# Attention and feed-forward on one core: the first batch's q and k loaded with four tokens in a partition and turned by their place in the group; SP's times in the planner's list as traced

## The chip, the core and the metric

The kernel runs on one core of one Trainium2 chip. The metric is the device time of one execution in microseconds, the median of several. A core has a matrix engine (TensorE, here PE, with its weight loads as PEld), VectorE (DVE), ScalarE (ACT), GpSimd (POOL), and SyncE (SP), which issues every DMA of this kernel. Each takes its instructions in the order of its own list. 16 DMA engines move the bytes. All operands are float32.

## The reference: what is computed

For each of 8 batches and 8 heads (576 tokens, head size 64), two attentions are added: one over q, k and v averaged over groups of four tokens (144 groups), whose result is repeated for the four tokens, and a local one in which a token sees the tokens at a distance below four. The sum, as rows of 512, goes through a layer norm and a feed-forward of 512 to 2048 to 512, and is added to the result.

```
q_d = q.reshape(B, H, Sd, 4, D).mean(axis=3)          # k_d, v_d likewise, Sd = 144
out_up = np.repeat(sm_attn(q_d, k_d, v_d), 4, axis=2)
mask = np.abs(pos[:, None] - pos[None, :]) < 4
out_local = softmax(where(mask, q @ k.T / sqrt(D), -1e9)) @ v
x = (out_up + out_local) as [B, S, H * D]
return x + relu(layernorm(x) * g_ln @ w_ch1) @ w_ch2
```

The two weight matrices arrive as 64-bit numbers and are turned into pairs of float32r tiles (hi and lo) on the chip.

## The kernel before, in words

**Stages.** The 4608 rows of x are cut into 18 chunks of 256 rows. A chunk is normed (`norm`), turned (px), split into xh and xlo, and then goes through 8 pairs of weight blocks (`ffn`): matmuls into h (L996), relu and split into hh and hl, matmuls into acc (L1019). The weights, 16 blocks of w1 and of w2, are loaded (L347, L352) and converted (cva, hi, lo) once, beside the first two chunks. Ahead of a chunk stands the attention of its batch: five windows of local attention (`local`, two strips of 58 tokens each, with overlap 64 rows), and four pairs of heads of pooled attention (`pooled_pair`).

**The first batch** (`own`, b = 0). Each of its five windows loads q and k as rows of tokens: for each, two DMAs of 64 rows with 8 runs of 256 bytes a row (`load_rows`, L428). PE turns a window with four transposes of 128x128 each (L458) into a PSUM tile, DVE adds groups of four columns there (`sums`, L480) into gsq and gsk, which are q and k of the pooled attention, and ACT copies the tile to SBUF (L465). Then come scores (ls), the softmax (lmx, la), its transpose (lt, at), the product with v (lv) and the division (xl). Pooled attention goes over qbdg, gs, gmx, ag, gt, agt and gv to od. Four tiles of x are made from xl and od by matmuls with 0/1 matrices (ex), and then normed. v of the pooled attention comes by its own loads (raw0v, raw1v: 72 rows, four heads with 1 KiB runs) and two additions on POOL; v of the windows goes into four tiles vwin. Windows 5 and 6 (of batch 1) use `load_rows` too; later ones use loads of blocks, DVE transposes, and moves of xl into x in pieces of up to 58 rows (L662).

**What sets the order.** `Plan` is given every step with an engine, a duration, what it depends on, a due time, and what it takes and gives of three kinds of rooms: SBUF tiles of 2 KiB a partition ("u", 88 of them), staging tiles and 8 PSUM banks ("a"). `order()` lists the steps as engines and rooms come free on its own clock, and the program is written out in that order, one list per engine; the durations in it order the work and do nothing else. T0, C1 and CHUNK set the due times of the feed-forward's pairs, W0 and W_GAP those of the weights, `rate` and `kb` the pace at which it believes bytes to land. Where the list leaves PE idle in its first 150 us, dummy transposes of the identity (L197) are put in.

Of the kernel before, what the change touches and what calls it, by code (L numbers as in the profile page):

```python
# [22 lines left out]
class Plan:  # L23
# [116 lines left out]
def attention_then_ffn(  # L140
# [129 lines left out]

    T0 = 35
    C1 = 5
    CHUNK = 55
    PACE = CHUNK / NPR

# [43 lines left out]
    U, A, STG = (("u", 1),), (("a", 1),), (("stg", 1),)  # L319
    DMA, LAT, W_AHEAD = 0.5, 2.9, 40  # L320

# [15 lines left out]
    def weights(which, f):  # L337
# [64 lines left out]
    chosen, own_moves = {}, []  # L402
    last_local = SimpleNamespace(v=[None] * NVW)

    def local(i):
# [44 lines left out]
        own = b < NPB  # L450
        for src, nm in ((q, "q"), (k, "k")):
            if by_pe:

                def turn(nm=nm):
                    p = psa(f"l{nm}{i}")
                    x.p[nm] = p
                    for pr in range(NPAIR):
                        nc.tensor.transpose(  # L458
                            p[:, pr * P : (pr + 1) * P],
                            x.raw[nm][:, 2 * pr : 2 * pr + 2].rearrange("p h d -> p (h d)"), ident,  # L460
                        )
# [6 lines left out]
                def sums(nm=nm):  # L468

                    for par in range(2):  # L470
                        t0 = window_start(w, par)
                        g0, g1 = (-(-(NQ * (2 * w + p)) // FACTOR) for p in (par, par + 1))
                        g1 = min(g1, SD)
                        c0 = 64 * par + FACTOR * g0 - t0
                        p = x.p[nm].rearrange("p (c t) -> p c t", c=NPAIR)
                        for hg in range(2):
                            key = (b, hg, nm)
                            if key not in gsum:
                                gsum[key] = unit([P, 2, SD], f"gs{nm}{b}_{hg}")
                            nc.vector.tensor_reduce(  # L480
                                out=gsum[key][:, :, g0:g1],
                                in_=p[:, 2 * hg : 2 * hg + 2, c0 : c0 + FACTOR * (g1 - g0)]
                                .rearrange("p c (g r) -> p c g r", r=FACTOR),
                                axis=AX.X, op=ALU.add,
                            )

                t = add("SP", 1.46, lambda src=src, nm=nm: load_rows(src, nm), (), due - 12.0, take=U,
                        lag=LAT, kb=256, ahead=AHEAD)
                t = add("PE", 0.43, turn, (t,), due - 8.0, take=A, give=U)
                if own:  # L490
                    t = add("DVE", 4 * dve(120), sums, [t] + gsum_done.get((b, nm), []), due - 8.0,
                            take=() if w else (("u", 2),))
                    gsum_done.setdefault((b, nm), []).append(t)
                turned.append(add("ACT", act(512), turn_out, (t,), due - 8.0, take=U, give=A))
            else:

                def turn(nm=nm):
                    t = unit([P, H, 64], f"l{nm}t{i}")
                    nc.vector.transpose(
                        t.rearrange("p h j -> p (h j)"), x.raw[nm].rearrange("p h j d -> p (h j d)")  # L500
                    )
                    setattr(x, nm + "t", t)

                ts = []
                for jb in range(2):
                    ts.append(add("SP", 4 * DMA, lambda src=src, nm=nm, jb=jb: load_blocks(src, nm, jb), ts,
                                  due - 14.0, take=() if jb else U, lag=LAT, kb=128, ahead=AHEAD))
                turned.append(add("DVE", dve(512), turn, ts, due - 8.0, take=U, give=U))
        vt = add("SP", 4 * DMA, load_v, (last_local.v[i % NVW],), due - 8.0, lag=LAT, kb=256, ahead=AHEAD)

        def scores_by_pair():
# [4 lines left out]
            for h2 in range(2):  # L516
                nc.tensor.matmul(
                    x.ps[h2], lhsT=ident_b, rhs=mask_b.unsqueeze(1).broadcast_to([P, NPAIR, 64]),
                    start=True, stop=False,
                )  # L520
            for pr in range(NPAIR):
                for h2 in range(2):
                    ds = slice(64 * h2, 64 * h2 + 64)
                    for par in range(2):
                        hs = slice(64 * par, 64 * par + 64)
                        nc.tensor.matmul(
                            x.ps[h2][hs, pr], lhsT=x.qt[ds, pr, hs], rhs=x.kt[ds, pr, hs],
                            start=False, stop=pr == NPAIR - 1,
# [77 lines left out]
        def divided(h2, eng):  # L606
# [7 lines left out]
            for pr in range(NPAIR):  # L614
# [3 lines left out]
        t = add("PE", 0.75, scores_by_pair if by_pe else scores_by_block, turned, due - 6.0,  # L618
                take=(("a", 2),), give=(("u", 2),))
        if not by_pe:  # L620
# [30 lines left out]
        for e, (n, p0, r0, m, par) in enumerate(moves):  # L651

            def move(n=n, p0=p0, r0=r0, m=m, par=par):
# [7 lines left out]
                for h2 in range(2):  # L661
# [4 lines left out]

            t = add("SP", DMA if by_pe else 2 * DMA, move, outs, due + 1.0, take=() if n in piece else U,
                    give=U if e == len(moves) - 1 else (), lag=LAT, kb=116)
# [13 lines left out]
    def pooled_half(b, hg):  # L682
# [6 lines left out]
        if own:  # L689
            ready["q"], ready["k"] = gsum_done[b, "q"], gsum_done[b, "k"]  # L690
        for nm, src in (("v", v),) if own else (("q", q), ("k", k), ("v", v)):
            for half in range(2):
# [23 lines left out]
                by_dve = b == 0 and nm == "k"  # L716
                t = add("SP", 0.82, load, (), due - 4.0, take=STG, lag=LAT, kb=288, ahead=AHEAD)
                t = add(
# [8 lines left out]
    def pooled_pair(b, hg, pr, x, ready):  # L727
# [121 lines left out]
        od_done.append(t)  # L849
        t = add("SP", DMA, keep, (t,), due, lag=LAT)  # L850
        ud_done.setdefault(b, []).append(t)
# [4 lines left out]
    def norm(n):  # L856
# [105 lines left out]
        else:  # L962
            t = add("SP", DMA * len(rows), load_up, [d for _, _, b, _ in rows for d in ud_done[b]], due - 4.0,
                    take=U, lag=LAT, kb=256, ahead=12.0)
# [95 lines left out]
    choice_done = plan.add("POOL", 4.0, make_choice, (), 10.0, take=U)  # L1060
    spread_done = plan.add("POOL", 2.5, make_spread, (choice_done,), 20.0, take=U)
    for i in range(NPB * NWIN):
        local(i)
# [52 lines left out]
```

## Time and profile before

| what | us |
|---|---|
| three runs: median, lowest, highest | 1064.73, 1063.45, 1066.62 |
| profiled execution, its own time | 1069.35 |
| span of its profile | 1067.0 |
| mean granted clock | 0.990 |

All views quoted below are of that one execution, in microseconds from the start of its span. Its own time is 2.35 us longer than the span and 4.62 longer than the median of the runs. The page cuts the span into 40 slices of 26.7 us; the digits are the busy share in tenths, PEclk the granted clock of TensorE:

```profile
PE   8897899989999999999999999999989999999998
DVE  7589954634353534444444443545434454534211
ACT  5575632413332222132222221223222222222110
PEclk9898999999999999999999999999999999999999
DMA  7788445535433533344354434243442443201000
GB/s 156 214 230 287 129 106 123 146 80 114 88 86 82 119 82 92 69 94 97 77 118 95 106 78 114 42 130 74 109 90 66 87 87 76 62 27 32 9 20 20
```

In a row of the groups, "out<-in" are the tiles written and read, behind the bar stand the busy time, the mean time of one in ns, and how long the engine had been idle just before, with what ended that. In the chain and the timeline a row gives start, length, engine, line, and how many instructions are merged.

### The profile page before, as it was taken

To read this page: it belongs to the slowest core of one execution; us is meant where nothing else is said; L and a number is where in the kernel's file an instruction comes from. 1 tells how busy PE (TensorE), PEld (TensorE's weight loads), DVE (VectorE), ACT (ScalarE), POOL (GpSimd) and SP (SyncE) were. 2 spreads that over 40 slices of the span, in tenths; PEclk is the share of its full clock that TensorE was granted. 3 is DMA by queue.
4 is the path that set the end of the run, shared out by engine and by line. 5 is a ranking of instruction groups with operands and counts; after the bars stand their busy time and mean duration, and the time that the engine had idled before them with its cause. 6 is when DMAs were issued, how large, how long until landed. Compare 5 with 4: busy or idle time off the path is not lost.

```text
span 1067.0 us, 23720 instructions
## 1 busy us (share of the span) xinstructions
PE 1039.3 (97%) x9280; PEld 932.2 (87%) x9280; DVE 509.5 (48%) x1307; ACT 313.2 (29%) x856; POOL 268.7 (25%) x286
## 2 busy tenths in 40 slices
PE   8897899989999999999999999999989999999998
PEld 8786789979999888889898989898989989888997
DVE  7589954634353534444444443545434454534211
ACT  5575632413332222132222221223222222222110
POOL 4233546323105221231224150142301400000000
PEclk9898999999999999999999999999999999999999
DMA  7788445535433533344354434243442443201000
GB/s 156 214 230 287 129 106 123 146 80 114 88 86 82 119 82 92 69 94 97 77 118 95 106 78 114 42 130 74 109 90 66 87 87 76 62 27 32 9 20 20
DMA packets 289295, 104.33 MB, mean 98 GB/s; under 512 B 237945, under 2 KB 276089, under 8 KB 289185
## 3 DMA queue, kind: packets, MB, share of 16 engines
q1 hardware_dynamic: 289185, 102.83, 40.7%
q8 instruction: 73, 1.20, 0.5%
q14 instruction: 37, 0.30, 0.1%
HBM read 82.58 MB, written 11.80 MB: 88 GB/s over the span
## 4 chain that ended last, share of the span: by engine, by line
PE 87%; DMA 4%; DVE 4%; SPq 2%; ACT 1%; issue 1%; POOL 0%; DVEq 0%; ACTq 0%; POOLq 0%
PE h L996 36%; PE acc L1019 35%; PE gv L802 3%; DMA s<-in_moe_w_ch_dram 3%; PE lv L596 2%; PE gs L766 2%; PE ls L540 2%; PE lt L575 1%; PE px L923 1%; PE gt L785 1%; SPq L428 1%; DVE cva L370 1%; DMA x<-xl 1%; PE gq L739 1%; DVE lo L383 1%
## 5 line engine op out<-in xcount | busy, mean ns | idle before, releaser
L1019 PE MATMUL acc<-hi,hl 128*128 128x512 f32 x576 | 238.2, 413 | 5.3 <-DVE hl L1007 5.3
L1019 PE MATMUL acc<-lo,hh 128*128 128x512 f32 x576 | 228.2, 396 | 0.0
L1019 PE MATMUL acc<-hi,hh 128*128 128x512 f32 x576 | 226.2, 393 | 0.0
L1003 ACT ACTIVATE hh<-h 128x512 fp32r<-128x512 f32 x144 | 86.2, 599 | 437.8 <-PE h L996 393.6
L1007 DVE SCALAR_TENSOR_TENSOR hl<-h,hh 128x512 fp32r<-128x512 f32 x144 | 98.9, 687 | 222.3 <-ACT hh L1003 214.7
L996 PE MATMUL h<-xh,lo 128*128 128x256 f32 x1152 | 193.2, 290 | 0.0
L996 PE MATMUL h<-xlo,hi 128*128 128x256 f32 x1152 | 185.3, 283 | 0.0
L996 PE MATMUL h<-xh,hi 128*128 128x256 f32 x1152 | 185.1, 283 | 0.0
L996 PEld LDWEIGHTS h<-xh,lo 128*128 128x128 f32 x1152 | 168.4, 190 | 16.9 <-POOL lo L383 0.2
L996 PEld LDWEIGHTS h<-xlo,hi 128*128 128x128 f32 x1152 | 159.1, 192 | 0.0
L996 PEld LDWEIGHTS h<-xh,hi 128*128 128x128 f32 x1152 | 158.6, 191 | 0.0
L896 POOL TENSOR_TENSOR x<-x,up 128x512 f32<-128x512 f32 x32 | 41.2, 1289 | 416.6 <-DMA x<-xl 310.9
L1019 PEld LDWEIGHTS acc<-hi,hh 128*128 128x128 f32 x576 | 109.0, 189 | 25.3
L1019 PEld LDWEIGHTS acc<-hi,hl 128*128 128x128 f32 x576 | 109.8, 191 | 22.0 <-DVE hl L1007 6.4
L1019 PEld LDWEIGHTS acc<-lo,hh 128*128 128x128 f32 x576 | 109.9, 191 | 12.5
L930 ACT ACTIVATE xh<-px,gain 128x128 fp32r<-128x128 f32 x144 | 43.6, 372 | 77.1 <-PE px L923 47.7
L940 DVE SCALAR_TENSOR_TENSOR xlo<-px,gain,xh 128x128 fp32r<-128x128 f32 x144 | 42.7, 344 | 34.7 <-ACT xh L930 34.5
L904 DVE BATCH_NORM_STATS2 st<-x 128x6 f32<-128x512 f32 x32 | 21.9, 686 | 47.1 <-POOL x L896 46.0
L779 ACT ACTIVATE ag<-gs,gmx 96x144 f32<-96x144 f32 x96 | 28.9, 373 | 42.9 <-DVE gmx L771 42.7
L1027 DVE SCALAR_TENSOR_TENSOR x<-acc,x 128x512 f32<-128x512 f32 x36 | 24.4, 688 | 35.3 <-PE acc L1019 35.3
L546 DVE TENSOR_TENSOR ls<-ls,mask 128x256 f32<-128x256 f32 x66 | 26.6, 424 | 27.2 <-PE ls L540 27.2
L802 PEld LDWEIGHTS gv<-vd,agt 72*72 72x72 f32 x512 | 37.2, 145 | 1.4
(191 smaller groups left out, 1156.8 us busy)
## 6 DMA issues: line engine op xcount, KB each, us to landing
s<-in_moe_w_ch_dram SPq DMA_DIRECT2D x64, 256.0 KB
vwin<-in_v_dram SPq DMA_DIRECT2D x160, 64.0 KB
out_dram<-x SPq DMA_DIRECT2D x36, 256.0 KB
qr<-in_q_dram SPq DMA_DIRECT2D x264, 32.0 KB
kr<-in_k_dram SPq DMA_DIRECT2D x264, 32.0 KB
up<-ud SPq DMA_DIRECT2D x28, 256.0 KB
x<-xl SPq DMA_DIRECT2D x66, 58.0 KB
ud<-od SPq DMA_DIRECT2D x32, 72.0 KB
```

The lines of the kernel that those rows point to most:

```text
L546: nc.vector.tensor_add(x.ps[n], x.ps[n], mask.unsqueeze(1).broadcast_to([P, NPAIR, 64]))
L779: nc.scalar.activation(y.a[:, c], y.ps[:, c], AF.Exp, scale=POOLED_SCALE, bias=y.mx[:, c : c + 1])
L802: nc.tensor.matmul(y.pv[:, qh, h2], lhsT=y.at[kh][:, h2, qh * GH : (qh + 1) * GH], rhs=vd[:, kh, 2 * pr + h2], start=kh == 0, stop=kh == 1,)
L896: nc.gpsimd.tensor_add(xt[n], xt[n], x.up)
L904: nc.vector.bn_stats(st, x.up if by_pe else xt[n])
L930: nc.scalar.activation(xh[c][i][:, k, j * P : (j + 1) * P], pxt[n][:, kc], AF.Copy, scale=gain[:, kc : kc + 1])
L940: nc.vector.scalar_tensor_tensor(out=xlo[c][i][:, k, ts], in0=pxt[n][:, kc], scalar=gain[:, kc : kc + 1], in1=xh[c][i][:, k, ts].bitcast(F ...
L996: nc.tensor.matmul(ph[c, p][:, fi], lhsT=wt[:, kc], rhs=xx[kc // 2][:, kc % 2], start=n == 0, stop=n == 3 * KC - 1)
L1003: nc.scalar.activation(hh[c, p], ph[c, p], AF.Relu)
L1007: nc.vector.scalar_tensor_tensor(out=hl[c, p].rearrange("p c t -> p (c t)"), in0=ph[c, p].rearrange("p c t -> p (c t)"), scalar=0.0, in1=h ...
L1019: nc.tensor.matmul(acc[c][j], lhsT=lt[:, fi, ts], rhs=rt, start=p == 0 and fi == 0 and n == 0, stop=p == NPR - 1 and fi == 1 and n == 2,)
L1027: nc.vector.scalar_tensor_tensor(out=x, in0=acc[c][j], scalar=1.0 + 2.0**-23, in1=x, op0=ALU.mult, op1=ALU.add)
```

## The change

**q and k of the first batch.** They are no longer loaded by window. `own_half` cuts the 144 groups of four tokens into two halves that overlap by three groups: groups 0 to 73 (74 of them) and 71 to 143 (73). For each pair of heads, each half, and each of q and k one DMA brings a group into a partition: 74 or 73 partitions, for each of two heads one run of 1 KiB (four tokens of 64). That makes 16 DMAs of 148 or 146 KiB where there were 20 of 128 KiB. PE turns the tile with eight matmuls against the identity, one for each place in the group and each head, written to PSUM at every fourth column, so that the tokens stand in order; DVE adds groups of four columns (288 at a time, to 72 sums), ACT copies 296 or 292 columns into an SBUF tile that stays until the last window that needs it. A window's scores then read 64 columns out of these tiles (`own_piece`). Each pooled half waits for the sums of its own four heads.

**The planner's numbers.** T0, CHUNK, W0, rate, LAT and the SP durations and sizes (kb) of all loads are set anew.

```
-        self.rate, self.moved = 245.0, 0.0
+        self.rate, self.moved = 260.0, 0.0
...
-    T0 = 35
+    T0 = 30
-    CHUNK = 55
+    CHUNK = 54
-    W0, W_GAP = 40, 13
+    W0, W_GAP = 30, 13
-    DMA, LAT, W_AHEAD = 0.5, 2.9, 40
+    DMA, LAT, W_AHEAD, W_LAG = 0.5, 2.5, 40, 1.5
...
-        t = add("SP", 2 * DMA, load, (), due, take=(("u", 3),), lag=LAT, kb=512, ahead=W_AHEAD)
+        t = add("SP", 1.3, load, (), due, take=(("u", 3),), lag=LAT + W_LAG, kb=512, ahead=W_AHEAD)
...
+    OWN_G = ((0, GH + 2), (GH - 1, SD))
+    def own_half(b, half):
+        g0, g1 = OWN_G[half]
+        ng = g1 - g0
+        for e, (nm, src, pr) in enumerate((nm, src, pr) for pr in range(NPAIR) for nm, src in (("q", q), ("k", k))):
...
+                x.raw = unit([P, 2, FACTOR, D], f"{nm}o{b}_{pr}_{half}")[:ng]
+                nc.sync.dma_start(
+                    x.raw.rearrange("p h r d -> p h (r d)"),
+                    src[b, 2 * pr : 2 * pr + 2, FACTOR * g0 : FACTOR * g1].rearrange("h (g r) d -> g h (r d)", r=FACTOR),
+                )
...
+                for r in range(FACTOR):
+                    for h2 in range(2):
+                        nc.tensor.matmul(
+                            x.p[64 * h2 : 64 * h2 + 64, :, r], lhsT=x.raw[:, h2, r], rhs=ident[:ng, :ng],
+                            start=True, stop=True,
+                        )
...
+            t = add("SP", 0.5, load, (), due - 4.0, take=U, lag=LAT, kb=147, ahead=AHEAD)
+            t = add("PE", 0.45, turn, (t,), due, take=A, give=U)
...
-        for src, nm in ((q, "q"), (k, "k")):
+        for src, nm in () if own else ((q, "q"), (k, "k")):
...
-            ready["q"], ready["k"] = gsum_done[b, "q"], gsum_done[b, "k"]
+            ready["q"], ready["k"] = list(gsum_done[b, hg, "q"]), list(gsum_done[b, hg, "k"])
```

**What moves in the lists.** First SP, from its first loads on; qn and kn are a window's q and k, qo and ko those of a pair of heads and a half (the first number is the pair, the second the half). Before:

```order
L428 DMA qn_111<-in_q_dram 64x8x64 x2
L428 DMA kn_114<-in_k_dram 64x8x64 x2
L428 DMA qn_139<-in_q_dram 64x8x64 x2
L428 DMA kn_155<-in_k_dram 64x8x64 x2
L428 DMA qn_173<-in_q_dram 64x8x64 x2
L428 DMA kn_197<-in_k_dram 64x8x64 x2
L428 DMA qn_215<-in_q_dram 64x8x64 x2
L428 DMA kn_249<-in_k_dram 64x8x64 x2
L428 DMA qn_272<-in_q_dram 64x8x64 x2
L428 DMA kn_309<-in_k_dram 64x8x64 x2
L700 DMA raw0v_332<-in_v_dram 72x4x256
L700 DMA raw1v_361<-in_v_dram 72x4x256
```

And of the change, from the fifth of the 16 loads on:

```order
L420 DMA qo_0_1_119<-in_q_dram 73x2x256
L420 DMA ko_0_1_143<-in_k_dram 73x2x256
L420 DMA qo_2_0_145<-in_q_dram 74x2x256
L420 DMA ko_2_0_164<-in_k_dram 74x2x256
L420 DMA qo_1_1_179<-in_q_dram 73x2x256
L420 DMA ko_1_1_194<-in_k_dram 73x2x256
L420 DMA qo_3_0_208<-in_q_dram 74x2x256
L420 DMA ko_3_0_222<-in_k_dram 74x2x256
L420 DMA qo_2_1_236<-in_q_dram 73x2x256
L420 DMA ko_2_1_248<-in_k_dram 73x2x256
L420 DMA qo_3_1_267<-in_q_dram 73x2x256
L420 DMA ko_3_1_282<-in_k_dram 73x2x256
```

The first four are qo and ko of pairs 0 and 1, half 0, 74 partitions each; behind the last stand the two raw0v, two vwin, raw1v, two more vwin around the other raw1v, and two blocks of w1, as before but for the place of the raw loads.

Second PE at the end of the first transposes. Before, the fifth window's transposes stand behind three windows' scores, and the pooled scores (gs) behind them:

```order
L458 MATMUL lq_365<-ident,qn_272 128x128 x4
L575 MATMUL lt_381<-ident,la_275 128x128 x4
L575 MATMUL lt_386<-ident,la_334 128x128 x4
L458 MATMUL lk_395<-ident,kn_309 128x128 x4
L517 LDWEIGHTS ident_b
```

In the change, 14 of the 16 transposes stand ahead of window 0's scores, and the last two ahead of the first gs:

```order
L429 MATMUL lq_2_1_328<-ident,qo_2_1_236 64x73 x8
L429 MATMUL lk_2_1_340<-ident,ko_2_1_248 64x73 x8
L557 LDWEIGHTS ident_b
L557 MATMUL ls_0_352<-mask_b,ident_b 128x256
...
L571 MATMUL ls_1_353<-okt_3_0_338,oqt_3_0_322 64x64 x2
L429 MATMUL lq_3_1_377<-ident,qo_3_1_267 64x73 x8
L429 MATMUL lk_3_1_388<-ident,ko_3_1_282 64x73 x8
L813 MATMUL gs_0_406<-gsk_0_190,qbdg_80 96x144 x3
```

So everything of PE but one window's scores stands behind the loads of half 1.

Third ACT, at the first conversions of weights (cva of block 0 of w2 reads s_0_0 and s_0_1; at feeds lv, x is a finished tile of x). Before:

```order
L582 COPY at_800<-lt_784 128x512
L359 ACTIVATE cva_0_819<-s_0_0_754 128x256
L359 ACTIVATE cva_0_819<-s_0_1_755 128x256
L900 COPY x_849<-ex_793 128x512
L378 CAST hi_0_856<-cva_0_668 128x512
L582 COPY at_868<-lt_851 128x512
```

In the change:

```order
L627 COPY at_858<-lt_841 128x512
L947 COPY x_900<-ex_850 128x512
L378 CAST hi_0_911<-cva_0_739 128x512
L627 COPY at_923<-lt_906 128x512
L359 ACTIVATE cva_0_928<-s_0_0_812 128x256
L359 ACTIVATE cva_0_928<-s_0_1_813 128x256
```

The conversion of w2's first block has moved behind x, hi and the last window's at.

More of the change, by code (lines that the diff above doesn't have):

```diff
@@ L466, in turn_out @@
                     setattr(x, nm + "t", t)
[L468 to L488, printed above, removed]
+                t = add("SP", 1.33, lambda src=src, nm=nm: load_rows(src, nm), (), due - 12.0, take=U,
+                        lag=LAT, kb=360, ahead=AHEAD)
                 t = add("PE", 0.43, turn, (t,), due - 8.0, take=A, give=U)
[L490 to L493, printed above, removed]
                 turned.append(add("ACT", act(512), turn_out, (t,), due - 8.0, take=U, give=A))
@@ L506, in local @@
                     ts.append(add("SP", 4 * DMA, lambda src=src, nm=nm, jb=jb: load_blocks(src, nm, jb), ts,
[L507 removed]
+                                  due - 14.0, take=() if jb else U, lag=LAT, kb=200, ahead=AHEAD))
                 turned.append(add("DVE", dve(512), turn, ts, due - 8.0, take=U, give=U))
[L509 removed]
+        if own:
+            for half in range(2):
+                if half in {int(window_start(w, par) + 64 > FACTOR * OWN_G[0][1]) for par in range(2)}:
+                    turned += own_done[b, half]
+            turned.append(last_local.ls)
+        vt = add("SP", 2.65 if own else 2.65, load_v, (last_local.v[i % NVW],), due - 8.0, lag=LAT, kb=360, ahead=AHEAD)
         def scores_by_pair():
@@ L618, in local @@
         t = add("PE", 0.75, scores_by_pair if by_pe else scores_by_block, turned, due - 6.0,
-                take=(("a", 2),), give=(("u", 2),))
+                take=(("a", 2),), give=() if own and w not in (2, NWIN - 1) else (("u", 2 * NPAIR if own else 2),))
+        if own:
+            last_local.ls = t
         if not by_pe:
@@ L665, in move @@
                     )
-            t = add("SP", DMA if by_pe else 2 * DMA, move, outs, due + 1.0, take=() if n in piece else U,
+            t = add("SP", 0.76 if by_pe else 2.0, move, outs, due + 1.0, take=() if n in piece else U,
                     give=U if e == len(moves) - 1 else (), lag=LAT, kb=116)
@@ L716, in pooled_half @@
                 by_dve = b == 0 and nm == "k"
-                t = add("SP", 0.82, load, (), due - 4.0, take=STG, lag=LAT, kb=288, ahead=AHEAD)
+                t = add("SP", 0.45, load, (), due - 4.0, take=STG, lag=LAT, kb=288, ahead=AHEAD)
                 t = add(
@@ L849, in pooled_pair @@
         od_done.append(t)
-        t = add("SP", DMA, keep, (t,), due, lag=LAT)
+        t = add("SP", 0.42, keep, (t,), due, lag=LAT)
         ud_done.setdefault(b, []).append(t)
@@ L962, in norm @@
         else:
-            t = add("SP", DMA * len(rows), load_up, [d for _, _, b, _ in rows for d in ud_done[b]], due - 4.0,
+            t = add("SP", 0.64 * len(rows), load_up, [d for _, _, b, _ in rows for d in ud_done[b]], due - 4.0,
                     take=U, lag=LAT, kb=256, ahead=12.0)
@@ L1061, in attention_then_ffn @@
     spread_done = plan.add("POOL", 2.5, make_spread, (choice_done,), 20.0, take=U)
+    for b in range(NPB):
+        for half in range(2):
+            own_half(b, half)
     for i in range(NPB * NWIN):
```

35 lines of the change are left out of this document (33 added, 2 removed).

## The prediction

> **What bounds the kernel now.** I read the page first: the busy line and the shares of the chain that ended last.
>
> ```profile
> span 1067.0 us, 23720 instructions
> PE 1039.3 (97%) x9280; PEld 932.2 (87%) x9280; DVE 509.5 (48%) x1307; ACT 313.2 (29%) x856; POOL 268.7 (25%) x286
> PE 87%; DMA 4%; DVE 4%; SPq 2%; ACT 1%; issue 1%; POOL 0%; DVEq 0%; ACTq 0%; POOLq 0%
> ```
>
> TensorE (PE) is busy for 97% of the span. So the end is set by when the feed-forward (L996 and L1019) starts, plus the PE work that stands behind that start, plus what PE idles behind it. The windows view splits this; the first three rows are of L996 alone, the last two of everything.
>
> ```profile
> 0.00:40.00 40.00, 0.00 (x0) 0.00 (x0) 1.00 0.71 163
> 40.00:60.00 20.00, 0.00 (x0) 0.00 (x0) 0.83 0.91 265
> 60.00:80.00 20.00, 9.67 (x72) 9.10 (x73) 1.00 0.78 209
> 62.00:140.00 78.00, 65.83 (x524) 56.38 (x523) 72.77 (x139) 49.52 (x132) 36.14 (x29) 0.96 0.67 194
> 140.00:1067.00 927.00, 917.43 (x8086) 826.24 (x8084) 395.96 (x1025) 228.75 (x627) 212.77 (x216) 1.00 0.37 83
> ```
>
> Columns of the last two: length, busy time of PE, PEld, DVE, ACT, POOL, granted clock, DMA share, GB/s. Until 62 us no feed-forward matmul runs. From 62 us on PE works 65.83 + 917.43 = 983.3 us and idles 1005 - 983.3 = 21.7 us, 12.2 of it before 140 us. Hence **end = first feed-forward matmul + 983 + idle**, and a shift of that first matmul reaches the end, less what of the 21.7 us it can swallow. What leads to that matmul is in the chain of waits and PE's timeline.
>
> ```profile
> 15.02 3.99 DMA kn<-in_k_dram
> ...
> 20.62 1.53 PE gs L197 x12
> ...
> 32.71 4.32 PE gv L802 x64
> ...
> 41.53 4.32 DMA s<-in_moe_w_ch_dram
> ...
> 47.83 1.24 PE lv L596 x31
> ```
> ```profile
> 62.12 0.72 PE L996 MATMUL h<-xh,lo 128*128 128x256 f32 x4
> ```
>
> The last k rows of batch 0 land at 15.02 + 3.99 = 19.0 us. Pooled attention ends on PE at 37.0 (32.71 + 4.32), there is one wait for weights (4.3 us), and the first feed-forward matmul starts at 62.1: 43.1 us behind the last landing, 18.0 of them up to the end of gv.
>
> **The change, part by part.** The loads first. Before, each of 10 loads of q or k is two DMAs of 64 token rows; now there are 16 DMAs, eight of 74 partitions and eight of 73, with runs of 1 KiB. Bytes: 8 x 74 x 2 KiB + 8 x 73 x 2 KiB = 2.41 MB against 20 x 128 KiB = 2.62 MB. The question is how many of the 16 DMA engines such a DMA uses. Three kinds of transfers in this trace tell it. First the loads of 64 rows, which are nearly all that moves from 3 to 16 us:
>
> ```profile
> DMA packets 9502, 2.38 MB, mean 183 GB/s; under 512 B 9501, under 2 KB 9501, under 8 KB 9501
> q1 hardware_dynamic: 9501, 2.36, 80.5%
> ```
>
> They keep 80.5% of 16 engines busy. Then a load of 72 rows with the very shape of the new ones (1 KiB runs of a four-token group), alone in the queue from 241.2 to 241.7 us:
>
> ```profile
> 239.31 0.36 SPq L700 DMA_DIRECT2D raw6q<-in_q_dram  x1
> ```
> ```profile
> DMA packets 139, 0.14 MB, mean 285 GB/s; under 512 B 0, under 2 KB 139, under 8 KB 139
> q1 hardware_dynamic: 139, 0.14, 79.9%
> ```
>
> 79.9% of 16 is 12.8; with packets overlapping a little, that fits 12 engines. Last, moves of 58 and of 46 rows (58.0 and 46.0 KB at 1 KiB a row) from 788.9 to 795.2 us:
>
> ```profile
> DMA  2000011110111111111111111111111111111597
> GB/s 60 0 0 0 11 37 36 37 36 23 36 36 37 34 37 36 36 37 36 36 36 36 36 36 37 36 37 36 36 36 37 34 36 37 36 37 36 62 153 206
> ...
> x<-xl SPq DMA_DIRECT2D x2, 58.0 KB
> x<-xl SPq DMA_DIRECT2D x2, 46.0 KB
> ```
> ```profile
> 790.75 5.30 DMA x<-xl
> ```
>
> For over 5 us one to two tenths of the engines are busy at a flat 36 GB/s, and the chain waits 5.30 us for it. Four DMAs (208 KB: 213 kB / 36 GB/s = 5.9 us) go one after another through the same two engines while 14 stand still. 64 = 4 x 16 rows get 16 engines, 72 = 6 x 12 get 12, 58 = 2 x 29 and 46 = 2 x 23 get two: **the number of engines divides the number of rows**. By that, 74 = 2 x 37 rows get two engines and 73, a prime, gets one. The Trainium skill says the same on the page "DMA: Bandwidth & Descriptors", section "Why a DMA increments its semaphore by 16 and not by 1": the engine count is the largest up to 16 that divides the slowest dimension of both sides, and the lowest-numbered ones are taken. The trace agrees for 64, 72, 58 and 46 rows; no run here has a prime count.
>
> The price: 285 GB/s over 12 engines is 23.8 GB/s for one engine with 1 KiB packets. A DMA of 74 rows puts 75.8 kB on each of two engines, 3.2 us; one of 73 rows puts 149.5 kB on one, 6.3 us. Eight of each in the queue of one engine: 8 x (3.2 + 6.3) = **76 us**. Bytes flow from about 3 us on, as the rows here show:
>
> ```profile
> 1.31 1.43 SPq L428 DMA_DIRECT2D qn<-in_q_dram  x2
> ...
> 13.63 2.02 SPq L428 DMA_DIRECT2D kn<-in_k_dram  x2
> ```
> ```profile
> 0.00:2.50 2.50, 1.00 (x4) 1.00 (x5) 1.42 (x3) 1.58 (x2) 1.69 (x12) 1.00 0.10 1
> ```
>
> So the last k lands at about 3 + 76 = 79 us in place of 19.0: **+60 us**. Bounds: if a 73-row DMA too ran on two engines, 8 x 3.2 + 8 x 3.1 = 50 us, landing at 53, +34. If an engine had only the 18 GB/s of the two-engine moves above, 76 x 23.8 / 18 = 100 us, +84; those packets are of 256 bytes, so I stay near the 1 KiB row.
>
> What stands behind the landing. The order puts all 16 transposes ahead of everything of batch 0 but the scores of window 0, so PE's list waits for the last pairs; ACT's 16 copies stand ahead of its first exponential, and no weight is converted before them. From the landing on, the same steps follow as before: softmax of pooled and local scores, gt, lv, gv. More stands there now: before, DVE had done three windows of local softmax when the last k came; now all four stand behind the last sums, each two L551 and two L556.
>
> ```profile
> L556 DVE TENSOR_TENSOR ls<-ls,lmx 128x256 f32<-128x256 f32 x8 | 3.0, 423 | 0.0
> L551 DVE TENSOR_REDUCE lmx<-ls 128x4 f32<-128x256 f32 x8 | 3.0, 418 | 0.0
> ```
>
> A window is 6.0 / 4 = 1.5 us of DVE (busy; the second operand overlaps), so at most +4.5 us for three. On the other side the dummy matmuls that stand in this stretch of the chain (1.53 us at gs, quoted above, and three lots at gt) shrink from 13 entries to 7 in PE's list, and the pooled maxima, on which gt and gv hang, stand between the windows in DVE's list, behind one and two of them: -3 us at best. I take 0 for the 18.0 us to the end of gv, with -3 and +4.5 as ends. v is behind q and k in the same queues; its pooling on POOL goes in two rounds of two items:
>
> ```profile
> L713 POOL TENSOR_TENSOR raw0v<-raw0v x2: 1265/1266/1266, 20.9 to 27.8; 72x512 f32<-72x512 f32 x2
> L714 POOL TENSOR_TENSOR vd<-raw0v x2: 724/725/726, 22.3 to 29.1; 72x256 f32<-72x256 f32 x2
> ```
>
> 4 x (1.27 + 0.73) = 8 us and one load between them, some 11 us, which ends beside the 18.
>
> Weights cannot use the 60 us. SP's list has the store of od (ud) ahead of all of w2, as before:
>
> ```profile
> 40.05 0.97 SPq L825 DMA_DIRECT2D ud<-od  x2
> 41.07 0.89 SPq L352 DMA_DIRECT2D s<-in_moe_w_ch_dram  x2
> ```
>
> od needs gv, so SP stands there until about 97 us with two of the 16 column blocks of w1 issued, and the weights come behind as before. One thing is better: ACT's list now has at (for lv) ahead of the first conversion of w2, so the 4.3 us wait at 41.53 holds less: -3 us.
>
> The rest is small. PE loses 40 transposes of 128x128 and gets 128 matmuls of 64x74:
>
> ```profile
> L458 PE MATMUL lq<-ident,qn 128*128 128x128 f32 x24 | 4.1, 300 | 0.2 <-DMA qn<-in_q_dram 0.2
> L526 PE MATMUL ls<-lkt,lqt 64*64 64x64 f32 x160 | 3.5, 224 | 0.0
> L480 DVE TENSOR_REDUCE gsk<-lk 128x30 f32<-128x120 f32 (+2 forms) x20 | 4.2, 270 | 1.5 <-PE lk L458 1.5
> ```
>
> By the first row a transpose is 0.17 us and 40 are 6.8; the nearest row for the new ones gives 128 x 3.5/160 = 2.8 us, and at a transpose's price it is 21.8. All but the last pairs' wait for DMA either way, so it costs -1 to +2. DVE's 40 sums (8.3 us) become 16 of 288 columns, about 0.45 each (7 us), ACT's copies stay some 6 us; both are beside the loads. SP issues 16 DMAs instead of 20 (0.65 us each, from the two rows of SP above): 3 us less, hidden by the same queue. T0, CHUNK, W0, rate and SP's costs only move entries of the order; PE is full behind 140 us, where a new order gains at most the 9.6 us idle there, and before it the stretch has DVE at 72.77 of 78 us with the same work to do. I take 3 us of the 21.7 as swallowed, with 0 and 15 as ends.
>
> Sum: +60 (landing) + 0 (to gv) - 3 (at ahead of cva) - 3 (idle swallowed) = **+54 us**. The profiled execution's span of 1067.0 becomes 1121. Its own time, 1069.35, is 4.6 above the median 1064.73 of the runs; carried over to that median the forecast is 1064.7 + 54 = **1119 us**.
>
> **The rivals.**
>
> *All engines carry the new loads (faster).* If the loads of 73 and 74 rows were spread as those of 64, at 23.8 GB/s an engine they would take 2.41 MB / (16 x 23.8) = 6.3 us, against 2.62 MB at 183 GB/s, 14.3 us, now; SP's 16 issues of 0.65 us end at 12 and a load lands some 2.8 us behind its issue (raw6q: issued at 239.31, its last bytes at 242), so q and k are there at 14 to 15 us, 5 earlier, and with the -3 and -3 of above the time is 1054. For it speaks that 1 KiB packets move faster: 23.8 GB/s an engine against 183 / (16 x 0.805) = 14.2 with 256 bytes. The Trainium skill has that too ("DMA: Bandwidth & Descriptors", "Specifications": line rate from 512 B up). Against it speak the two-engine moves, whose packets waste no less. It decides from 8 engines a DMA on.
>
> *Two engines for both halves (slower, but less).* +34 in place of +60: 1064.7 + 34 - 6 = 1093.
>
> *The delay is swallowed.* If SP could load all weights within the 60 us, the 15 us of idle would go in place of 3: +42, 1107. Against it: the place of ud in SP's list. This lies inside the range. That it makes no difference at all would need 60 us of slack where there are 21.7.
>
> *The price is higher.* An engine alone at 18 GB/s: +84 - 6 = +78, 1143.
>
> **How the numbers follow.** Divisor rule with one queue, 1105 to 1143: 0.82. Both halves on two engines, about 1093: 0.08. All engines, about 1054: 0.07. No difference (spread over some 4 to 6 engines): 0.03. A measurement of this kernel tells 0.3%, 3 us, from no change, so faster 0.07, same 0.03, slower 0.90. The range leaves out the faster case and no difference; it goes from 1088 (1093 less 5 of idle) to 1143. The time is that of the likeliest case, 1119.
>
> **What would show it.** In the profile after: the DMA row of the 40 slices near 1 to 2 tenths with 25 to 50 GB/s up to 70 or 80 us, L429 on PE spread over that time and waiting for DMA qo and ko; the first L1043 at 115 to 122 us; from there on PE nearly full; SP standing before ud (L872). If L429 is done by 15 us, the divisor rule fails for these loads and with it the forecast; if it is done by 55, the prime count does not go to one engine; if the first L1043 is late but the end is not, the weights were loaded meanwhile.

## The result, and the profile after

The changed kernel takes 1128.01 us (median of 4 runs, 1126.85 to 1129.84) against 1065.29 of the kernel before on the same chip (4 runs, 1063.45 to 1066.62): a ratio of 1.0578, with an interval of 1.0554 to 1.0601. It is 62.7 us slower. The profiled execution took 1129.84 us, its span 1128.1, so the spans stand 61.1 us apart.

The page of the changed kernel, its busy line and the shares of the chain that ended last, and from the 40 slices PE, the granted clock, the DMA engines and what they moved:

```profile
PE 1048.7 (93%) x9466; PEld 938.6 (83%) x9466; DVE 510.4 (45%) x1279; ACT 316.9 (28%) x878; POOL 267.4 (24%) x286
...
PE   3339987899999999999999999999999999999998
...
PEclk9999998999999999999999999999999999999999
DMA  1027973635354434434344344325443333310000
GB/s 33 33 60 206 296 208 111 159 83 144 61 118 102 97 86 107 90 83 103 76 85 109 85 105 97 86 44 138 93 100 69 89 67 80 83 30 28 9 20 19
...
PE 78%; SPq 7%; DVE 6%; DMA 5%; issue 2%; ACT 1%; POOL 0%; ACTq 0%; DVEq 0%; POOLq 0%
```

PE does 9.4 us more work (1048.7 against 1039.3) in a span that is 61.1 us longer. The loss stands in the first three slices of 28 us: PE at three tenths, the DMA engines at one tenth, under one and two tenths, with 33 to 60 GB/s, where the kernel before had 156, 214 and 230. From the fourth slice on PE is at seven tenths or more, and at nine in nearly every slice. In the chain SP's share is 7% in place of 2%.

When does the feed-forward start, and what stands behind it? The windows view, first L1043 alone (PE, PEld, granted clock, DMA share, GB/s), then all engines:

```profile
120.00:140.00 20.00, 10.36 (x72) 9.41 (x72) 1.00 0.94 289
...
121.00:200.00 79.00, 67.97 (x558) 59.56 (x557) 77.56 (x151) 51.02 (x135) 34.20 (x28) 0.96 0.68 194
200.00:1128.00 928.00, 916.94 (x8072) 823.77 (x8070) 392.43 (x1011) 231.26 (x640) 213.38 (x217) 1.00 0.36 83
```

No feed-forward matmul runs up to 120.9 us. Behind the start PE works 67.97 + 916.94 = 984.9 us and idles 79 + 928 - 984.9 = 22.1, against 983.3 and 21.7 before. So the stretch behind the start is what it was, and the start itself has moved. The chain of waits (start, length, what) tells from where:

```profile
9.38 2.99 SPq L420
12.41 5.90 SPq L420
18.36 6.42 SPq L420
...
62.16 18.46 DMA ko<-in_k_dram
...
97.77 4.30 PE gv L849 x64
```

Up to 62 us the chain is one row after another of SP issuing a load, each held by the load ahead of it: 3.0 to 3.3 us where that has 74 partitions, 5.9 to 6.4 where it has 73 (the three rows from 9.38 on are loads five to seven of the list, of 73, 73 and 74 partitions, behind loads of 74, 73 and 73). Then comes the last load itself. It lands at 62.16 + 18.46 = 80.6 us (19.0 before); gv ends at 102.1 (37.0). PE's timeline, with the wait ahead of a row in brackets, shows the two ends of that stretch:

```profile
80.76 1.24 PE L429 MATMUL lk<-ident,ko 73*64 73x73 f32 x16 [5.86 <-DMA ko<-in_k_dram]
81.93 3.20 PE L813 MATMUL gs<-gsk,qbdg 128*96 128x144 f32 x12
...
120.92 0.72 PE L1043 MATMUL h<-xh,lo 128*128 128x256 f32 x4
```

And the DMA view from 20 to 60 us, one column a microsecond:

```profile
DMA  0000111111111000000000001111111000000000
GB/s 25 24 25 25 40 30 37 49 48 46 49 47 39 24 25 24 25 25 24 25 25 24 25 25 33 40 49 48 46 48 48 32 24 25 25 24 25 24 25 25
DMA packets 1253, 1.29 MB, mean 32 GB/s; under 512 B 12, under 2 KB 1252, under 8 KB 1252
```

Two levels alternate: 24 to 25 GB/s, and 46 to 49. The first is one DMA engine (a load of 73 partitions), the second is two (74). Hardly a packet is small: the counts in the last row are cumulative, so 1240 of 1253 have 512 bytes to 2 KB and 12 have less. Only engines are lacking.

### The profile page after: what moved, and what is told of

Its sections match the earlier page's. It is cut to its first block, busy times and chain, and to the rows that moved or that the text cites. A ratio compares the mean times of both kernels' runs of the same rounds, so it can differ in the third digit from the quotient of the medians.

```text
span 1128.1 us, 24156 instructions
## 1 busy us (share of the span) xinstructions
PE 1048.7 (93%) x9466; PEld 938.6 (83%) x9466; DVE 510.4 (45%) x1279; ACT 316.9 (28%) x878; POOL 267.4 (24%) x286
## 4 chain that ended last, share of the span: by engine, by line
PE 78%; SPq 7%; DVE 6%; DMA 5%; issue 2%; ACT 1%; POOL 0%; ACTq 0%; DVEq 0%; POOLq 0%
PE h L1043 33%; PE acc L1066 32%; SPq L420 5%; PE gv L849 3%; PE lv L641 2%; PE gs L813 2%; PE ls L585 2%; DVE cva L370 2%; DMA ko<-in_k_dram 2%; PE lt L620 1%; DMA s<-in_moe_w_ch_dram 1%; DVE cva L367 1%; PE px L970 1%; PE gt L832 1%; DMA x<-xl 1%
## 5 line engine op out<-in xcount | busy, mean ns | idle before, releaser
L1043 PE MATMUL h<-xh,lo 128*128 128x256 f32 x1152 | 193.8, 291 | 0.0
L1043 PE MATMUL h<-xlo,hi 128*128 128x256 f32 x1152 | 185.7, 284 | 0.0
L1043 PE MATMUL h<-xh,hi 128*128 128x256 f32 x1152 | 185.2, 283 | 0.0
L1043 PEld LDWEIGHTS h<-xh,lo 128*128 128x128 f32 x1152 | 168.6, 190 | 16.6
L1043 PEld LDWEIGHTS h<-xlo,hi 128*128 128x128 f32 x1152 | 159.3, 192 | 0.2
L1043 PEld LDWEIGHTS h<-xh,hi 128*128 128x128 f32 x1152 | 158.6, 191 | 0.0
L370 DVE SCALAR_TENSOR_TENSOR cva<-s,cva 128x256 int32<-128x256 int32 x64 | 40.0, 665 | 1.1
L1074 DVE SCALAR_TENSOR_TENSOR x<-acc,x 128x512 f32<-128x512 f32 x36 | 24.3, 686 | 32.6 <-PE acc L1066 32.6
L849 PE MATMUL gv<-vd,agt 72*72 72x65 f32 x512 | 38.0, 228 | 0.5 <-DVE od L866 0.5
```

The lines of the kernel that those rows point to most:

```text
L370: nc.vector.scalar_tensor_tensor(out=a, in0=x.raw[i].rearrange("p (n two) -> p n two", two=2)[:, :, 0], scalar=29, in1=a, op0=ALU.logical_ ...
L849: nc.tensor.matmul(y.pv[:, qh, h2], lhsT=y.at[kh][:, h2, qh * GH : (qh + 1) * GH], rhs=vd[:, kh, 2 * pr + h2], start=kh == 0, stop=kh == 1,)
L1043: nc.tensor.matmul(ph[c, p][:, fi], lhsT=wt[:, kc], rhs=xx[kc // 2][:, kc % 2], start=n == 0, stop=n == 3 * KC - 1)
L1074: nc.vector.scalar_tensor_tensor(out=x, in0=acc[c][j], scalar=1.0 + 2.0**-23, in1=x, op0=ALU.mult, op1=ALU.add)
```

## The experiments

The theory: a DMA is spread over the largest number of engines up to 16 that divides its partitions, an engine gives 23.8 GB/s here, and each microsecond by which the last k lands later moves the end by one. Against it stand: the new way of turning q and k (more and smaller matmuls, longer tiles) or the new order costs the time; or it is loads with 1 KiB runs, or of heads in pairs, that are slow as such. The numbers of the planner are a part of their own.

**The same transfers, cut in two.** Each load becomes one DMA of 64 partitions and one of the 10 or 9 that are left; order, tiles and matmuls stay.

```diff
-                nc.sync.dma_start(x.raw..., src[b, 2*pr : 2*pr+2, FACTOR*g0 : FACTOR*g1]...)
+                for c0, c1 in ((0, 64), (64, ng)):
+                    nc.sync.dma_start(x.raw[c0:c1]..., src[b, 2*pr : 2*pr+2, FACTOR*(g0+c0) : FACTOR*(g0+c1)]...)
```

> The changed kernel with each of its 16 first loads cut into two DMAs, 64 rows and the other 10 or 9; the order of every other instruction stays. Theory (the number of engines divides the rows, and the loads queue on the lowest-numbered ones): 64 rows get 16 engines, 10 and 9 get 10 and 9; SP's 32 issues at 0.65 us take 21 us, so the last k lands at about 25 us in place of 80.6, the last transposes end at 26 in place of 82.0, and the time is 1128 - 56 = 1072. Rival (the new order, the narrow transposes or the 1 KiB runs cost the time): the time stays at 1110 to 1128.

1069.27 us, ratio 1.0039 (1.0026 to 1.0053). Some 59 of the 62.7 us are gone with nothing changed but how the same bytes are cut into DMAs. PE's timeline has the last tile here:

```profile
24.31 1.24 PE L432 MATMUL lk<-ident,ko 73*64 73x73 f32 x16
```

24.3 in place of 80.8 us, and no wait for a DMA in brackets: the tiles now come nearly as fast as PE turns them here. The matmuls, the sums, the order and the 1 KiB runs are those of the changed kernel, so none of them is the cause of the 60 us.

**The fault put into the kernel before.** Its own loads of 64 rows are cut into 62 + 2 rows, for the first batch, and nothing else.

```diff
-                    x.raw[nm][64 * par : 64 * par + 64], src[b, :, t0 : t0 + 64, :]...
+                for c0, c1 in ((0, 62), (62, 64)) if b < NPB else ((0, 64),):
+                    x.raw[nm][64*par + c0 : 64*par + c1], src[b, :, t0 + c0 : t0 + c1, :]...
```

> The kernel before, every instruction in its old place, but each of the first batch's 20 row loads of q and k cut into 62 rows and 2 rows. Theory: 62 = 2 x 31 rows get two engines, 63.5 kB on each in 256-byte runs, at 14 to 18 GB/s an engine 3.5 to 4.5 us a load, 71 to 90 us for 20 in one queue; the last k lands at 75 to 93 us in place of 19, and the time is 1065 + 56 to 74, plus some 2 us for a PE that was idle: 1121 to 1141. Rival (the time is lost in the new order, not in the count of rows): 1065 to 1075.

1121.01 us, ratio 1.052 (1.0489 to 1.0551), at the lower edge of what was expected. The DMA view from 5 to 11 us:

```profile
DMA packets 854, 0.22 MB, mean 36 GB/s; under 512 B 854, under 2 KB 854, under 8 KB 854
```

62 = 2 x 31, and the 256-byte packets now flow at the flat 36 GB/s of the moves of 58 and 46 rows in the prediction. The last k lands at 76.5 us, inside the 75 to 93 of the expectation. So the fault needs nothing of the new code: 64 rows cut unluckily bring the old kernel to nearly the same time.

**A ladder of partition counts.** Only the borders of the halves change; the halves overlap more, so each step moves slightly more bytes.

```diff
-    OWN_G = ((0, GH + 2), (GH - 1, SD))      # 74 and 73 groups
+    OWN_G = ((0, n), (SD - n, SD))           # n = 74, 75, 76, 79 or 80
```

> Both halves with 74 groups: no prime count. Theory: 74 = 2 x 37 rows get two engines, 16 x 3.2 = 51 us, the last k lands at 54 in place of 80.6, time 1128 - 26.6 = 1101. Rival (the engines' choice rotates, or a prime count is no worse than 74): within 5 us of 1128, or near 1072.

> Both halves with 76 groups. Theory: 76 = 4 x 19 rows get four engines, 38.9 kB on each, 1.64 us a load, 16 in 26 us: the last k lands at 29, the first feed-forward matmul starts some 41 us behind it at 70, time about 1128 - 51 = 1077. Rival (between two engines and all of them there is nothing): 1063 or 1103.

> Both halves with 79 groups, one fewer than in e2_rows80 (1063 us). Theory: 79 is a prime, so one engine carries each of the 16 loads, 161.8 kB at 23.8 GB/s, 6.8 us: the last k lands at 3 + 109 = 112 us in place of 80.6 of the change, time 1128 + 31 = 1159. Rival (the engine count goes by halving or by size, a prime is not special): within 10 us of 1063, or of the 1103 of two engines.

> Both halves with 75 groups, one more than the wider half of the change. Theory (largest divisor up to 16): 75 = 5 x 15 rows get 15 engines, so as with 80: 1070 to 1072. Rival (only multiples of 16, or even numbers, are spread): one engine or few, 16 x 6.5 us, time over 1140.

> Both halves with 80 groups (0 to 79 and 64 to 143). Theory: 80 = 5 x 16 rows get all 16 engines; SP's 16 issues end at 12 us and the last k lands at about 15. Then PE sets the pace: 16 pairs of tile transposes at 1.24 us, 19.8 us from about 4 us on, so the last one ends at 24 to 26 in place of 82.0; time 1070 to 1072. Rival of before (all engines, and the earlier landing counts in full): first feed-forward matmul at 55, time 1054 to 1060. Rival (order or narrow transposes cost the 60 us): 1110 and more.

The GB/s are means of the DMA view from 5 to 11 us, for the change the two levels of the view above; the worked-out landing is 3 us plus 16 loads, each of its bytes by the engines times 23.8 GB/s; beside it stands the start of the last tile on PE, which is the first instruction behind that landing.

| partitions | engines that divide them | GB/s | landing worked out | last tile turned at | first feed-forward matmul | median us | ratio (interval) |
|---|---|---|---|---|---|---|---|
| 79 | 1 | 24 | 112 | 112.5 | 152.1 | 1158.76 | 1.0894 (1.0868 to 1.0920) |
| 74 and 73 (the change) | 2 and 1 | 25 and 48 | 79 | 80.8 | 120.9 | 1128.01 | 1.0578 (1.0554 to 1.0601) |
| 74 | 2 | 48 | 54 | 55.7 | 95.7 | 1103.08 | 1.0361 (1.0341 to 1.0380) |
| 76 | 4 | 96 | 29 | 31.8 | 71.9 | 1078.07 | 1.0136 (1.0104 to 1.0167) |
| 75 | 15 | 247 | 10 | 15.5 | 54.8 | 1062.63 | 0.9987 (0.9966 to 1.0009) |
| 80 | 16 | 257 | 10 | 16.3 | 55.8 | 1063.04 | 0.9993 (0.9968 to 1.0018) |

From 74 partitions to 76, two more, the time falls by 25 us; from 75 to 76, one more, it rises by 15; from 76 to 79 by 81. No cost by size, by bytes or by matmuls goes up and down like that; the divisor does. And the landing as worked out is met within 3 us on the four rungs that wait for it. Between those rungs (76, 74, the change, 79) the last tile's start moves by 23.8, 25.1 and 31.8 us and the median by 25.0, 24.9 and 30.8: next to nothing is swallowed, all the way from 32 us to 113. Below that the landing is no longer what comes last, but PE's own work on the 16 tiles, and the rungs with 15 and 16 engines meet.

The DMA views from 5 to 11 us of three rungs side by side, first 79, then 76, then 80 partitions; the last figure of the second row is the share of 16 engines:

```profile
DMA packets 142, 0.14 MB, mean 24 GB/s; under 512 B 1, under 2 KB 142, under 8 KB 142
...
q1 hardware_dynamic: 142, 0.14, 6.8%
```
```profile
DMA packets 579, 0.58 MB, mean 96 GB/s; under 512 B 16, under 2 KB 579, under 8 KB 579
...
q1 hardware_dynamic: 579, 0.58, 27.2%
```
```profile
DMA packets 1638, 1.54 MB, mean 257 GB/s; under 512 B 147, under 2 KB 1637, under 8 KB 1637
...
q1 hardware_dynamic: 1637, 1.53, 100.2%
```

6.8% of 16 is 1.1 engines, 27.2% is 4.4, and 100.2% is all of them. The two prime counts, 73 and 79, were the open end of the prediction: both get one engine. That is also what the Trainium skill says of 127 partitions ("DMA: Bandwidth & Descriptors", "Why a DMA increments its semaphore by 16 and not by 1"), and the trace agrees with its rule on 73, 74, 76 and 79. 75 and 80 partitions keep 98.3% and 100.2% of 16 engines busy, which does not tell 15 engines from 16.

The expectation for 75 and 80 partitions was 7 us too slow: it had the tiles turned at the 1.24 us apiece of the changed kernel. With 80 partitions PE does one in 0.55 to 0.6 us, as the starts in its timeline show; the last of 16 starts at 16.3 us. (The 1.24 us are those of a halved clock; the last section shows it.)

```profile
8.42 0.72 PE L429 MATMUL lk<-ident,ko 80*64 80x80 f32 x16
8.98 0.72 PE L429 MATMUL lq<-ident,qo 80*64 80x80 f32 x16
...
16.33 0.72 PE L429 MATMUL lk<-ident,ko 80*64 80x80 f32 x16
```

**The planner's numbers alone, and the new loads alone.** First the kernel before with T0, CHUNK, W0, rate, LAT and SP's times of the change; then 80 partitions with the numbers of before.

```diff
 (the kernel before)                      (80 partitions)
-    T0 = 35                              +    T0 = 35
+    T0 = 30                              -    T0 = 30
...
```

> The kernel before with only the planner's numbers of the change (T0, CHUNK, W0, rate, LAT, SP's durations and kb); loads and transposes of the first batch stay those of before. Theory (the 63 us are the price of the few engines alone): within 4 us of before, 1061 to 1069. Rival (the new numbers order the weights worse and cost a part): 1072 or more.

> 80 groups a half as in e2_rows80, with the planner's numbers of before. Theory (numbers hardly matter, PE is full behind 140 us): within 4 us of e2_rows80, 1059 to 1067. Rival (the new numbers are worth the lead of 5 us in e2_rows80's profile, or cost it): 1068 or more, or 1058 or less.

Both theories missed, by 5 us each and in opposite directions; 80 partitions came out where the second rival has them. The numbers alone give 1056.25 (ratio 0.9922, 0.9896 to 0.9948), a gain of 9 us; 80 partitions with the old numbers give 1072.24 (1.0063, 1.0038 to 1.0088). The four corners:

| median us | numbers of before | numbers of the change | difference |
|---|---|---|---|
| loads of before, 64 rows | 1065.3 | 1056.3 | -9.0 |
| loads of the change, 80 partitions | 1072.2 | 1063.0 | -9.2 |
| difference | +6.9 | +6.8 | |

The two parts add up within the noise of a corner: the numbers are worth 9 us with either kind of load, and the new loads, with all 16 engines, cost 7 us with either set of numbers. What the counts of 74 and 73 cost is the rest: 1128.0 - 1063.0 = 65 us.

Where do the 7 us lie? With the change's numbers the first feed-forward matmul starts at 56.3 with the old loads and at 55.8 with the new ones, so not ahead of it. The windows view from there to the end of the span, first the numbers alone, then 80 partitions (PE is the first busy column, DVE the third):

```profile
56.30:200.00 143.70, 136.58 (x1148) 123.22 (x1147) 107.21 (x223) 75.86 (x215) 72.17 (x64) 0.98 0.66 181
200.00:1054.30 854.30, 847.85 (x7497) 760.73 (x7495) 358.34 (x934) 207.75 (x565) 177.88 (x182) 1.00 0.35 79
```
```profile
55.80:200.00 144.20, 131.49 (x1097) 117.80 (x1096) 112.00 (x223) 73.82 (x207) 64.24 (x57) 0.96 0.60 162
200.00:1061.60 861.60, 852.71 (x7534) 765.44 (x7532) 359.35 (x938) 208.40 (x568) 183.85 (x188) 1.00 0.35 80
```

PE's work is the same, 984.4 and 984.2 us. It idles 7.1 + 6.5 = 13.6 us with the numbers alone and 12.7 + 8.9 = 21.6 with 80 partitions (21.7 before). That is the difference, and most of it lies ahead of 200 us, where the weights are converted. The groups of DVE from 50 to 200 us (busy time and mean ns behind the bar), first the numbers alone, then 80 partitions:

```profile
L370 DVE SCALAR_TENSOR_TENSOR cva<-s,cva 128x256 int32<-128x256 int32 x62 | 36.9, 635 | 1.1
L367 DVE TENSOR_SCALAR cva<-cva 128x512 int32<-128x512 int32 x31 | 15.9, 512 | 0.0
```
```profile
L370 DVE SCALAR_TENSOR_TENSOR cva<-s,cva 128x256 int32<-128x256 int32 x62 | 40.4, 693 | 1.1
L367 DVE TENSOR_SCALAR cva<-cva 128x512 int32<-128x512 int32 x31 | 19.3, 622 | 0.0
```

The same 93 conversions hold DVE for 52.8 us in one and 59.7 in the other, 7 us more. Why they are longer, the traces tell: in both, every conversion above 440 ns (19 of the 93 in one, 27 in the other) overlaps an instruction of POOL, and each that overlaps none takes 408 to 427 ns. So it goes by when POOL works beside them. DVE with 80 partitions, two conversions beside two instructions of POOL (L383 and L760, from 73.97 to 76.76) and two with POOL idle:

```profile
74.21 2.84 DVE L370 SCALAR_TENSOR_TENSOR cva<-s,cva 128x256 int32<-128x256 int32 x2
77.96 0.76 DVE L370 SCALAR_TENSOR_TENSOR cva<-s,cva 128x256 int32<-128x256 int32 x2
```

Whether this makes the 7 us stays open. The kernel before has 52.4 us for these conversions and still idles 21.7, so they cannot be the whole of it, and no run took it apart.

**Is the gain of the numbers chance?** A list scheduler gives another list for each number. T0 was set to 31 in place of 30, in both kernels with the change's numbers.

```diff
-    T0 = 30
+    T0 = 31
```

> e2_rows80 with T0 31 in place of 30, which moves due times by 1 us and so some places in the lists. Theory (the 7 us between e2_rows80, 1063, and e5_numbers, 1056, belong to one order of the list and not to the loads): it moves by 3 us or more, either way. Rival (the 80-group loads themselves cost 7 us): 1061 to 1065.

> e5_numbers with T0 31 in place of 30. Theory (its 9 us lead over before is one lucky order): it gives back 3 us or more, 1059 to 1067. Rival (the new numbers are better as such): 1054 to 1058.

80 partitions go from 1063.04 to 1059.83 (ratio to before 0.9972, 0.9945 to 1.0000; 6 runs), and the numbers alone from 1056.25 to 1054.29 (0.9910, 0.9890 to 0.9930). By the medians that is 3.2 and 2.0 us, and in both pairs the intervals overlap, so neither move is clear of the noise; a difference of 2 to 3 us between two lists says nothing about the edit. The 9 us hold: the numbers alone stay in the range of the rival and gain in both settings. The price of the new loads is 5.5 us here, so "5 to 7" is as sharp as these runs make it. The last kernel, loads and windows of before with the planner's numbers and T0 at 31, has the lowest median of this study and is faster than both kernels.

**Half as many matmuls to turn a tile.** 80 partitions, with the tile laid out so that the two heads stand side by side: four matmuls of 128 columns in place of eight of 64. The runs of the loads become 256 bytes.

```diff
-                    for h2 in range(2):
-                        nc.tensor.matmul(x.p[64*h2 : 64*h2+64, :, r], lhsT=x.raw[:, h2, r], rhs=ident[:ng, :ng], ...)
+                    nc.tensor.matmul(x.p[:, :, r], lhsT=x.raw[:, r].rearrange("p h d -> p (h d)"), rhs=ident[:ng, :ng], ...)
```

> 80 groups a half as in e2_rows80, and the tile laid out so that two heads of a token stand together: four transposing matmuls of 80x128 a tile in place of eight of 80x64, and DMA runs of 256 bytes in place of 1 KiB. Theory (the landing sets the pace, the transposes run beside): 2.62 MB at 227 GB/s (the rate of the old row loads) land by 15 us, so within 3 us of e2_rows80, 1060 to 1066. Rival (the transposes set the pace, 16 x 0.55 us in e2_rows80): 4 to 5 us faster, 1058.

1077.64 us (1.0129, 1.0084 to 1.0173): a miss, 15 us slower than 80 partitions as they were. The loads are not late. PE is: its timeline has the tiles back to back at 1.71 us each (the starts of two rows; a row's length overlaps the next),

```profile
25.48 1.92 PE L429 MATMUL lq<-ident,qo 80*128 80x80 f32 x8
27.18 1.91 PE L429 MATMUL lk<-ident,ko 80*128 80x80 f32 x8
```

and the last of the 16 ends at 34 us; the first feed-forward matmul starts at 72.1. A row is eight pieces, that is two for each matmul of the code, so there are half as many of them as before, and each takes 213 ns against 0.55 us / 16 = 34. That is not the price of the layout alone. Rows whose shape did not change are slow in the same stretch too: a window's scores (L571) take 1.13 us at 29.45 and 0.69 at 40.08, the first 12 gs 3.11 us and the next 12 1.71. PE as a whole was at half speed up to 38 us (last section). What the wide matmuls cost at full speed, no run shows.

## Why the prediction was right, point by point

**What bounds the kernel: right.** "End = first feed-forward matmul + 983 + idle" holds in the changed kernel with 984.9 and 22.1, and on the rungs of the ladder, where the first L1043 and the median move together: 71.9 to 95.7 to 120.9 to 152.1 against 1078 to 1103 to 1128 to 1159.

**How many engines: right, and shown.** 73 partitions on one engine and 74 on two, as worked out from loads of 64 and 72 rows and moves of 58 and 46. The cut into 64 + 10 or 9 takes the cost away, the cut into 62 + 2 brings it into the kernel before.

**The price: right.** 23.8 GB/s for an engine with 1 KiB packets, from the load of 72 rows; measured 24 to 25, and 24, 48 and 96 GB/s for one, two and four. 76 us from 3 us on gave 79 for the landing; it was 80.6, so +61.6 in place of +60.

**From the landing to the end of gv: 0 was too low by 3.4 us**, inside its bounds of -3 and +4.5. The bound of +4.5 came from DVE's windows. At least 2 us of what was measured have another source: PE, after waiting 5.9 us for the last tile, turns it in 1.24 us against 0.63 for the last four transposes before, and does the first 12 gs in 3.20 us against 1.71 in the kernel with 80 partitions. With the loads cut in two the same rows take 1.24 and 3.19 us, and there the trace has the clock at one half (last section).

**From gv to the first feed-forward matmul: -3 was too small; it is -6.2** (120.9 - 102.1 = 18.8 against 25.1). The direction was read right off ACT's list: the chain has no wait for weights in this stretch any more, where it had 4.3 us. That the wait cost as much again in slow work behind it wasn't foreseen. PE's timeline of before at the end of that wait, the windows view just behind it (granted clock third from the right), and the first of the same ex in the changed kernel:

```profile
47.83 1.24 PE L596 MATMUL lv<-vwin,at 64*64 64x65 f32 x32 [3.20 <-ACT at L582]
49.01 2.07 PE L884 MATMUL ex<-xl,choice 128*128 128x256 f32 x4
```
```profile
49.00:51.00 2.00, 2.00 (x7) 1.64 (x6) 1.85 (x7) 1.35 (x4) 0.34 (x1) 0.50 0.94 229
```
```profile
110.25 1.13 PE L931 MATMUL ex<-xl,choice 128*128 128x256 f32 x4
```

Before, PE idles 3.2 us and then does lv and the next 12 ex, at a granted clock of 0.50, in 6.3 us (47.83 to 54.15); in the change the same take 3.3 us (109.62 to 112.94). 3.2 + 3.0 = 6.2, the whole term.

**Idle swallowed: -3 was wrong in sign.** Idle went from 21.7 to 22.1 and PE's work from 983.3 to 984.9; with the exact starts (62.12 and 120.92) that is +2.3. Here the step failed that said the planner's numbers "only move entries of the order" and are worth 3 us of idle at most likely. They are worth 9 us of the median by themselves. Between the two profiled executions, whose spans are 12.7 apart, 5.8 come from a start at 56.3 in place of 62.1 and 8.1 from idle (13.6 in place of 21.7), less 1.1 of more work. The start's part came through in the changed kernel, within the -6.2 above: from the end of gv to the first feed-forward matmul there are 25.1 and 25.3 us with the numbers of before (loads of before, 80 partitions), and 20.6, 18.9 and 18.8 with those of the change (loads of before, 80 partitions, the change). The idle's part did not: with 80 partitions the new loads have 21.6 us of idle, 8.0 more than the loads of before with the same numbers. So a gain and a loss of some 8 us each, which the prediction both left out, stood against each other in the changed kernel. That the idle came out only 5.3 us from what was taken is luck.

**The sum:** 61.6 + 3.4 - 6.2 + 2.3 = 61.1, the difference of the spans, where the prediction had 60 + 0 - 3 - 3 = 54. Of the 7 us between them the idle makes 5.3, gv 3.4, the landing 1.6, and the weights -3.2.

**SP before ud: right in effect, wrong in cause.** The weights did not use the 60 us, but not because SP stood before ud (L872): there it waited 0.6 us at most at a time, for gr, lr or od. SP could not get there. It was held by its own issues of the loads up to 68 us and then by v's, and reached the first blocks of w1 at 90.6 us. The prediction had SP's issues of the loads at 0.65 us, "hidden by the same queue". They were 3.0 to 6.4 us each from the third on. It changed nothing in the sum, since the queue was the bound either way; with a second user of SP in that time it would have.

**The rivals.** All engines: this is now the kernel with 80 partitions, and it takes 1063.0, not 1054, as the new loads have that price of 5 to 7 us, most of it behind the start. Two engines for both halves: that is 74 partitions, 1103.1 against the 1093 worked out; it fell 10 short for the same terms (idle, gv), and because the landing was at 55 and not at 53. Delay swallowed: refuted by the ladder, where each microsecond of delay was one of the end. Higher price: refuted by 24 GB/s.

## What to carry to other kernels

Read the partition count of a DMA as a divisor problem before its size: the largest divisor up to 16 is the number of engines it gets, and a prime above 16 gets one. Here 80 partitions instead of 74 and 73, with 9% more bytes, took back 65 us in a line of code. When an edit brings two parts, run the four corners: here a gain of 9 us from a table of numbers was hidden under a loss of 72. And move one number of a list scheduler by one before you read a meaning into 3 us.

## What the runs showed of the hardware that was not expected

**A full engine holds the issuer.** SP's time for one load, issued and not waited for, follows the number of engines of the load ahead of it: 0.44 us with 80 partitions, 1.61 with 76, 2.9 to 3.4 with 74, 6.70 with 79. Where 74 and 73 alternate, in the change, it is the count of the load ahead that tells: 3.0 to 3.3 us behind 74, 5.9 to 6.4 behind 73, whatever the load itself has. SP's timeline with 79 partitions and with 80:

```profile
25.75 6.70 SPq L420 DMA_DIRECT2D ko<-in_k_dram  x1
```
```profile
5.26 0.44 SPq L420 DMA_DIRECT2D qo<-in_q_dram  x1
```

Behind the first loads, which go out quickly, the issue takes as long as the engines need for a whole load (with 79 partitions 161.8 kB / 23.8 = 6.8 us). So a DMA on one engine also delays every later DMA of the same issuer, even those that would go to the 15 engines that stand still.

**PE at half speed where the view shows a full clock.** The changed kernel turns a tile of 16 small matmuls in 1.24 us, the kernel with 80 partitions in 0.55, and the windows view gives both a granted clock of 1.00. The run with the loads cut in two has both speeds, and there the view tells them apart. Two of its tiles, and the window around the second:

```profile
4.97 0.73 PE L432 MATMUL lq<-ident,qo 74*64 74x74 f32 x16
11.58 1.25 PE L432 MATMUL lq<-ident,qo 74*64 74x74 f32 x16
```
```profile
10.00:20.00 10.00, 8.80 (x131) 8.11 (x130) 3.66 (x8) 2.40 (x7) 0.26 (x1) 0.50 0.42 126
```

The shape is the same; the clock is not. Its trace records 1.00 from 4.7 us, 0.50 from 8.1 and 1.00 from 28.6, and up to there a window's scores take 1.13 us and the first 12 gs 3.19. Those are the times of the changed kernel up to 85 us, and of the kernel with half as many matmuls up to 38. In these two traces the first clock record stands at 85.3 and at 37.8 us, just where PE becomes fast. Ahead of it there is none, and the view shows 1.00 where it has no record. So 1.00 early in a span is no proof of a full clock; the time of a row whose shape is known is. The runs with 74 partitions say the same: three of the four have a mean granted clock of 0.972 or 0.973 and one has 0.997, and all take 1101.5 to 1103.9 us.

The Trainium skill describes a clock that is halved after an idle window and released after about 3.4 us of sustained work ("TensorE: Matmul & The Clock Gate", "Part 1: The HAM clock gate"). The trace agrees with the halving in the kernel before, where the record of 0.50 begins at 47.2 us, in the wait of 3.2 us. It doesn't in the run with the loads cut in two, where the clock falls at 8.1 us behind waits of 0.56 and 0.43 us only. The release came 3.1 to 3.8 us behind the start of the first gs in that run, the changed kernel and the one with half as many matmuls; but in the last, 24 us of wide transposing matmuls without a gap had not brought it. Which work counts, these runs do not show.
